# First token group of an attention-and-MLP kernel: order written out by hand, identity products ahead of it, first weights moved ahead of the last tokens

## The chip, the cores and the metric

The kernel runs on one core of one Trainium2 chip. The metric is the device time of one launch in microseconds (us). Three runs of the kernel before gave 675.87, 676.16 and 676.73 us; the median is 676.16 us. All positions below are microseconds from the start of the span of one profiled execution.

## The reference

A linear attention with decay (4 batches, 8 heads, 768 tokens, 64 columns per head) feeds a two-layer block on 3072 tokens (512 to 2048 to 512):

```python
for b in range(nb):                                   # blocks of tokens
    intra = einsum(qb, kb) * Dmask;  intra = einsum(intra, vb)
    inter = einsum(qb * lam_pow, kv_state)
    out[block] = intra + inter
    kv_state = lam_block * kv_state + einsum(kb * rev_pow, vb)
x = out as (B*S, H*D)
h = x @ w_in;  g = h - tanh(h);  result = g @ w_out
```

q, k, v are 32-bit floats. The weights arrive as 64-bit words and are turned into 32-bit floats on the chip.

## The kernel before, in words

The 768 tokens of each batch are cut into six groups of 128 (`g`); one group holds 4 batches x 128 = 512 tokens. A pair (g, b) is called a chunk here. Group 0 is done plainly; the later groups use schemes with fewer products, whose factors are built while group 0 runs. The change touches group 0 only.

**Loads (SP's queue).** `load_natural` (L123) issues q, k and v of a chunk, 256 KB each; chunk (0,3) is loaded in the order q, v, k. `load(B)` (L273) puts all four chunks of group 0 into the queue, then `load_weights(WAHEAD)` (L274) puts the first four blocks of `w_in`, 512 KB each: blocks 0 and 1 as one DMA each (L199), blocks 2 and 3 as two halves each (L202). Four buffers (`raw64`) hold raw blocks, so a later block is issued when the rounding of an earlier one has read its buffer. q has 2 buffers, k 3, v 4.

**Attention of a chunk.** `att_transpose` (L285): four TensorE transposes of q and four of k into two PSUM banks (`tp`), each copied out by ScalarE (`qt`, `kt`, L299). `att_scores` (L306): eight products into two banks (`sp`), then two VectorE multiplies by the decay mask (`ss`, L317). `att_state` (L320), for two chunks: VectorE scales k in place (L328), sixteen products (`kv`, L333), one ScalarE copy (`state`, L340). `att_out` (L342), for two chunks: sixteen products (`op`, L364) into two banks, then two ScalarE copies to `xt` (L368). `xt[0, 0]` holds chunks 0 and 1, `xt[0, 1]` chunks 2 and 3. All these use one ring of four PSUM banks (`att`).

**Rounding of a weight block.** `round_block` (L251) is two ScalarE operations, `r` (L261) and the absolute value into `w` (L263), then four VectorE operations: a maximum (L264), a shift with a mask (L266), the sign (L268), and the addition of `r` (L270). `r` has two buffers.

**The first layer.** `up_plain(u, c)` (L722), for unit u of 512 hidden columns and quarter c, sums the four input tiles i into one PSUM bank. Input tile i of unit u is weight block 4u + i. Quarters 11 and 21 read `xt[0, 0]`; 12 and 22 read `xt[0, 1]`. Sixteen quarter-steps follow, then the second layer `down_plain` (L736) with parts of group 1's attention in between.

**Order.** A scheduler sets each engine's order from the program; only operations given to `tc.keep_in_program_order` stay where they are written. In group 0 nothing is kept. Every engine works through its own queue strictly in that order. As built, TensorE's order before is:

```
tp(0,0) sp(0,0) tp(0,1) kv(0,0) sp(0,1)x2 kv(0,1) sp(0,1)x6 op(0,1)x10
tp(0,2)q x1 op x6 tp(0,2) rest, sp(0,2) tp(0,3) kv(0,2) sp(0,3)x1 kv(0,3) sp(0,3)x7
op(2,3)x10 h x1 op(2,3)x6 h ...
```

Of the kernel before, what the change touches and what calls it, by code (L numbers as in the profile page):

```python
# [23 lines left out]
def kernel(  # L24
# [90 lines left out]

    lam_blk = fwd[:, :, BLK - 1:BLK][:, None, :, :].to_broadcast([128, 2, NP, D])


    raw, late = {}, {}
    chunks = [(g, b) for g in range(NG) for b in range(B)]  # L120
    at = {"loaded": 0}

    def load_natural(g, b, names):  # L123
        for name, src, bufs in (("q", q, 2), ("v", v, 4), ("k", k, 3)) if (g, b) == (0, B - 1) else (
                ("q", q, 2), ("k", k, 3), ("v", v, 4)):
            if name in names:
                x = (qpool if name == "q" else io).tile([128, H, D], F32, name=f"{name}_nat", tag=name, bufs=bufs)
                op = nc.sync.dma_start(out=x, in_=src[b, :, ts(g, BLK), :].rearrange("h s d -> s h d"))
                if g >= GB:
                    tc.keep_in_program_order(op)  # L130
                raw[g, b][name] = x

    def load_blocks(g, b, names):
# [57 lines left out]
    ready = {"loaded": 0, "done": 0}  # L191
    wraw, pair = {}, {}

    def load_block(eng, dst, kind, n, m):

        if kind == "out":
            eng.dma_start(out=dst, in_=moe_w_out[ts(m * KH + n, 128), :].rearrange("k (a n) -> k a n", a=2))  # L197
        elif m < 2:
            eng.dma_start(out=dst, in_=w_in_u[ts(m, 128), :, ts(n, 256)])  # L199
        else:  # L200
            for j in range(2):
                eng.dma_start(out=dst[ts(1 - j, 64)], in_=w_in_u[ts(2 * m + j, 64), :, ts(n, 256)])  # L202

    def load_weights(n):

        while ready["loaded"] < min(n, len(blocks)):
            if moe_w_in.dtype != F32:
                raw64 = stage.tile([128, 2, 256], I64, name="raw64", tag="raw64", bufs=WAHEAD)
                block = blocks[ready["loaded"]]
                load_block(nc.sync if block[0] == "in" else nc.gpsimd, raw64, *block)  # L210
                wraw[ready["loaded"]] = raw64
            ready["loaded"] += 1

    def weights(n):

        while ready["done"] < min(n, len(blocks)):
            at_ = ready["done"]
            load_weights(at_ + WAHEAD)
            kind, n_, m = blocks[at_]
            if kind == "out" and m == 0:  # L220
                pair[n_] = wst.tile([128, 8, 256], F32, name="wt", tag="w")
            w = w1[n_][:, m] if kind == "in" else pair[n_][:, 2 * m:2 * m + 2]
            if at_ in wraw:
                round_block(w, wraw.pop(at_))
            else:
                load_block(nc.gpsimd, w, kind, n_, m)
            ready["done"] += 1
# [20 lines left out]
            nc.gpsimd.dma_start(out=fine[:, SUB.index(x), :, kt // 2, :].rearrange("n p c -> p n c"),  # L248
                                in_=wt[:, 3:8, ts(j, 128)])

    def round_block(w, raw64):  # L251


        word = raw64.rearrange("p a n -> p (a n)").bitcast(U32).rearrange("p (n w) -> p n w", w=2)
        wordf = raw64.rearrange("p a n -> p (a n)").bitcast(F32).rearrange("p (n w) -> p n w", w=2)
        lo, hi = word[:, :, 0], word[:, :, 1]
        w = w.rearrange("p a n -> p (a n)")
        wb, wi = w.bitcast(U32), w.bitcast(I32)

        r = stage.tile([128, 512], I32, name="r", tag="r", bufs=2)  # L260
        nc.scalar.activation(r, lo, AF.Copy, scale=2.0 ** -29)  # L261

        nc.scalar.activation(w, wordf[:, :, 1], AF.Abs)  # L263
        nc.vector.tensor_scalar(out=w, in0=w, scalar1=CLAMP, scalar2=None, op0=AL.max)  # L264

        nc.vector.tensor_scalar(out=wb, in0=wb, scalar1=3, scalar2=0x3FFFFFF8, op0=AL.logical_shift_left,  # L266
                                op1=AL.bitwise_and)
        nc.vector.scalar_tensor_tensor(out=wb, in0=hi, scalar=0xC0000000, in1=wb, op0=AL.bitwise_and,  # L268
                                       op1=AL.bitwise_or)
        nc.vector.tensor_tensor(wi, wi, r, op=AL.add)  # L270


    load(B)  # L273
    load_weights(WAHEAD)  # L274


    state = const.tile([128, B, NP, D], F32)

    def bank(name, tag, bufs):
        return psum.tile([128, 512], F32, name=name, tag=tag, bufs=bufs)  # L280


    tr, sc, kdec, xt = {}, {}, {}, {}
# [1 line left out]
    def att_transpose(g, bs):  # L285
        for b in bs:
            load(g * B + b + 1)
            t = raw[g, b]
            qt = work.tile([128, NP, BLK], F32, name="qt", tag="qt")
            kt = work.tile([128, NP, BLK], F32, name="kt", tag="kt")  # L290
            for dst, x in ((qt, "q"), (kt, "k")):
                if g >= GB:
                    tc.keep_in_program_order(nc.vector.transpose(out=dst.rearrange("d p i -> d (p i)"),
                                                                 in_=t[x + "b"].rearrange("d p r a -> d (p r a)")))
                else:
                    tp = bank("tp", "att", 4).rearrange("d (p s) -> d p s", p=NP)
                    for p in range(NP):
                        nc.tensor.transpose(out=tp[:, p, :], in_=t[x][:, 2 * p:2 * p + 2, :], identity=ident)  # L298
                    nc.scalar.activation(dst, tp, AF.Copy)  # L299
            qd = None  # L300
            if g > 0:
                qd = work.tile([128, NP, BLK], F32, name="qd", tag="qd")
                nc.vector.tensor_tensor(qd, qt, fwd, op=AL.mult)
            tr[g, b] = (qt, kt, qd)

    def att_scores(g, bs):  # L306
        for b in bs:
# [2 lines left out]
            sp = [bank("sp", "att", 4).rearrange("s (p i) -> s p i", p=NP) for _ in range(2)]  # L310
            for p in range(NP):
                for j in range(2):
                    nc.tensor.matmul(out=sp[j][:, p, :], lhsT=kt[ts(j, 64), p, :], rhs=qt[ts(j, 64), p, :],  # L313
                                     start=True, stop=True)
            ss = work.tile([128, 2, NP, BLK], F32, name="ss", tag="ss")
            for j in range(2):
                nc.vector.tensor_tensor(ss[:, j], sp[j], mask[:, j], op=AL.mult)  # L317
            sc[g, b] = ss

    def att_state(g, bs):  # L320
        if g == NG - 1:
# [2 lines left out]
        kv = bank("kv", "att", 4).rearrange("d (b p e) -> d b p e", b=2, p=NP)  # L324
        for n, b in enumerate(bs):
            kd, vn = raw[g, b]["k"], raw[g, b]["v"]
            kp = kd.rearrange("s (p j) d -> s p j d", j=2)
            kd_op = nc.vector.tensor_tensor(kp, kp, bwd, op=AL.mult)  # L328
            if g >= GB:
                tc.keep_in_program_order(kd_op)  # L330
            for p in range(NP):
                for j in range(2):
                    nc.tensor.matmul(out=kv[ts(j, 64), n, p, :], lhsT=kd[:, 2 * p + j, :], rhs=vn[:, 2 * p + j, :],  # L333
                                     start=n == 0 and p == 0, stop=True, skip_group_check=True)
        st = state[:, bs[0]:bs[0] + 2]
        if g > 0:
            nc.vector.tensor_tensor(st, st, lam_blk, op=AL.mult)
            nc.vector.tensor_tensor(st, st, kv, op=AL.add)
        else:
            nc.scalar.activation(st, kv, AF.Copy)  # L340

    def att_out(g, bs):  # L342
        half = bs[0] // 2
# [16 lines left out]
        for n, b in enumerate(bs):  # L360
            ss, vn = sc.pop((g, b)), raw[g, b]["v"]
            for p in range(NP):
                for j in range(2):
                    nc.tensor.matmul(out=dst(n, p, j), lhsT=vn[:, 2 * p + j, :], rhs=ss[:, j, p, :],  # L364
                                     start=g == 0 and n == 0 and p % 2 == 0, stop=n == 1 and p % 2 == 1,
                                     skip_group_check=True)
        for x in range(2):
            nc.scalar.activation(xt[g, half][:, 2 * x:2 * x + 2, :].rearrange("d p (b s) -> d p b s", b=2), ops[x], AF.Copy)  # L368

    def att_sums(g, bs):  # L370
        x0, x1 = xt[g, 0], xt[g, 1]
# [347 lines left out]
            nc.sync.dma_start(out=rows[:, m, c0:c1], in_=o[:, m, c0:c1])  # L719


    def up_plain(u, c):  # L722
        a, t = divmod(c - 11, 10)
        h = bank("h", ("ya", "yb", "z", "w")[2 * t + a], 1)
        hm = h.rearrange("q (m c) -> q m c", m=2)
        for m in range(2):
            for i in range(KI):
                nc.tensor.matmul(out=hm[:, m, :], lhsT=w1[u][:, i, a, ts(m, 128)], rhs=xt[0, t][:, i, :],  # L728
                                 start=m == 0 and i == 0, stop=i == KI - 1, skip_group_check=True)
        th = work.tile([128, 2, HB], F32, name="th", tag="th")  # L730
        nc.scalar.activation(th, hm, AF.Tanh)
        nc.vector.tensor_tensor(hidden(0, c)[:, u], hm, th, op=AL.subtract)

    obank = {}

# [17 lines left out]
        for fn, *args in pieces:  # L753
            fn(*args)

    for bs in ((0, 1), (2, 3)):
        for b in bs:
            att_transpose(0, (b,))
            if b == 3:
                weights(1)  # L760
            if b % 2:
                att_state(0, bs)
            att_scores(0, (b,))
        if bs[0]:
            weights(2)
        att_out(0, bs)
    weights(KI)
    for u in range(NU):
        for c in (11, 21, 12, 22):
            up_plain(u, c)  # L770
            weights(ready["done"] + 1)
        if u == 1:
            powers()
    p0, p1 = attention(1)
# [112 lines left out]
```

## Time and profile before

| what | value |
|---|---|
| median of 3 runs | 676.16 us (675.87 to 676.73) |
| time of the profiled execution | 674.97 us |
| its span, first to last instruction | 673.2 us |
| TensorE busy | 661.3 us (98% of the span) |
| VectorE, ScalarE, GpSimd busy | 481.1, 194.9, 199.9 us |
| mean granted TensorE clock | 1.000 |

Read the busy time as an average over very different stages: the first 26 us hold group 0's attention, where all engines wait for loads and for each other, and the rest is products back to back. One `nc.tensor.matmul` in 32-bit floats appears as two rows in the trace, for example 256 rows of `h` for 128 calls; a transpose appears as one row.

### The profile page before, as it was taken

The numbers are of one execution on the slowest core, as the hardware profiler recorded it, in microseconds if no ns is written. First come the engines' busy times: TensorE is split into PE (matmuls) and PEld (weight loads), VectorE is DVE, ScalarE is ACT, GpSimd is POOL, SyncE is SP. The second block draws the span as 40 slices with busy tenths as digits, with TensorE's granted clock in tenths as the row PEclk, the third lists the DMA queues.
The fourth block names the chain that finished last, engine by engine and source line by source line (L and its number), as shares of the span: only waits on it lengthen the run. The fifth ranks groups of instructions, "written<-read, shape, count | busy, mean of one in ns | idle before, by whom it ended". The sixth has DMA issues, their size and how long they took to land.

```text
span 673.2 us, 12843 instructions
## 1 busy us (share of the span) xinstructions
PE 661.3 (98%) x4808; PEld 574.9 (85%) x4808; DVE 481.1 (71%) x872; ACT 194.9 (29%) x373; POOL 199.9 (30%) x345
## 2 busy tenths in 40 slices
PE   6899999999999999999999999999999999999998
PEld 5788855558888999988999988899988899988897
DVE  3797858894887872399896378888358978347753
ACT  2764432423321111333112343112333112334110
POOL 0001414216432334144355200254300244400251
PEclk9999999999999999999999999999999999999999
DMA  9869978958855878487998741598840676610385
GB/s 187 228 210 238 288 216 256 298 145 253 264 140 125 240 200 214 115 246 214 250 281 255 198 82 44 148 284 243 250 83 5 153 244 200 231 48 0 110 302 168
DMA packets 162717, 128.80 MB, mean 191 GB/s; under 512 B 133856, under 2 KB 135008, under 8 KB 162656
## 3 DMA queue, kind: packets, MB, share of 16 engines
q0 software_dynamic: 28976, 96.49, 44.5%
q1 hardware_dynamic: 133536, 31.50, 23.5%
q8 instruction: 38, 0.62, 0.4%
q14 instruction: 23, 0.19, 0.1%
q10 hardware_dynamic: 144, 0.00, 0.0%
HBM read 103.55 MB, written 24.38 MB: 190 GB/s over the span
## 4 chain that ended last, share of the span: by engine, by line
PE 95%; DMA 2%; issue 1%; DVE 1%; ACT 0%; SPq 0%; POOL 0%; POOLq 0%; DVEq 0%
PE y L415 16%; PE y L677 11%; PE z L415 10%; PE h L728 8%; PE op L744 8%; PE zw L677 8%; PE w L624 5%; PE y L624 5%; PE y L499 4%; PE sp L313 3%; PE plain L624 3%; PE op L364 3%; PE z L499 2%; PE op L358 1%; PE kv L333 1%; PE tp L298 1%
## 5 line engine op out<-in xcount | busy, mean ns | idle before, releaser
L589 POOL DMA_DIRECT2D wb<-fine x147 | 79.2, 539 | 113.3 <-PE y L677 48.5
L423 ACT ACTIVATE th<-g 128x512 f32<-128x512 f32 x76 | 47.6, 630 | 98.7 <-DVE g L428 33.2
L592 POOL DMA_DIRECT2D wb<-factors x56 | 30.2, 541 | 153.9 <-PE y L624 97.3
L415 PE MATMUL y<-xt,w 128*128 128x256 f32 x320 | 74.0, 380 | 0.0
L415 PEld LDWEIGHTS y<-xt,w 128*128 128x128 f32 x320 | 59.9, 190 | 9.0 <-ACT g L503 0.9
L424 DVE TENSOR_TENSOR g<-g,th 128x512 f32<-128x512 f32 x76 | 51.9, 689 | 18.2 <-ACT th L423 18.1
L680 ACT ACTIVATE q<-y 128x128 f32<-128x128 f32 x84 | 23.3, 278 | 128.7 <-PE y L677 127.0
L744 PE MATMUL op<-wt,g 128*128 128x512 f32 x128 | 56.5, 595 | 0.0
L728 PE MATMUL h<-xt,w 128*128 128x256 f32 x256 | 56.1, 381 | 0.0
L728 PEld LDWEIGHTS h<-xt,w 128*128 128x128 f32 x256 | 48.3, 190 | 7.3 <-issue 0.3
L677 PE MATMUL y<-wb,g 128*128 128x128 f32 x384 | 51.1, 278 | 0.0
L744 PEld LDWEIGHTS op<-wt,g 128*128 128x128 f32 x128 | 23.8, 190 | 27.7 <-issue 26.5
L677 PEld LDWEIGHTS y<-wb,g 128*128 128x128 f32 x384 | 46.4, 192 | 1.2 <-issue 0.3
L415 PE MATMUL z<-xt,ws 128*128 128x256 f32 x160 | 38.0, 380 | 0.0
L415 PE MATMUL z<-tt,ws 128*128 128x256 f32 x160 | 38.0, 380 | 0.0
L415 PE MATMUL y<-tt,ws 128*128 128x256 f32 x160 | 37.8, 379 | 0.0
L317 DVE TENSOR_TENSOR ss<-sp,mask 128x512 f32<-128x512 f32 x48 | 31.0, 684 | 8.4 <-PE sp L313 8.4
L624 PE MATMUL y<-wb,g 128*128 128x256 f32 x160 | 35.6, 379 | 0.5 <-DVE g L434 0.5
L197 POOL DMA_DIRECT2D raw<-in_moe_w_out_dram x16 | 8.8, 553 | 91.5 <-DMA raw<-in_moe_w_in_dram 53.3
L624 PE MATMUL w<-wb,g 128*128 128x256 f32 x160 | 35.8, 382 | 0.0
L624 PEld LDWEIGHTS y<-wb,g 128*128 128x128 f32 x160 | 30.3, 190 | 5.0 <-PE y L415 0.9
L415 PEld LDWEIGHTS z<-xt,ws 128*128 128x128 f32 x160 | 30.2, 190 | 4.7 <-DVE g L446 0.4
(169 smaller groups left out, 1301.4 us busy)
## 6 DMA issues: line engine op xcount, KB each, us to landing
wb<-fine POOLq DMA_DIRECT2D x147, 256.0 KB, 3.8
wb<-factors POOLq DMA_DIRECT2D x68, 256.0 KB, 4.1
raw<-in_moe_w_out_dram POOLq DMA_DIRECT2D x16, 512.0 KB, 5.1
v_nat<-in_v_dram SPq DMA_DIRECT2D x24, 256.0 KB, 5.6
factors<-wt POOLq DMA_DIRECT2D x8, 768.0 KB, 5.5
wb<-fine_in POOLq DMA_DIRECT2D x24, 256.0 KB, 4.1
k_nat<-in_k_dram SPq DMA_DIRECT2D x20, 256.0 KB, 5.2
raw<-in_moe_w_in_dram SPq DMA_DIRECT2D x8, 512.0 KB, 5.5
```

What stands on the lines that cost most here:

```text
L317: nc.vector.tensor_tensor(ss[:, j], sp[j], mask[:, j], op=AL.mult)
L415: nc.tensor.matmul(out=t[:, m, :], lhsT=wt[:, kt, ts(m, 128)], rhs=x[:, kt, :], start=first and m == 0 and kt == 0, stop=kt == 1, skip_gro ...
L423: nc.scalar.activation(th, src, AF.Tanh)
L424: nc.vector.tensor_tensor(dst(c), src, th, op=AL.subtract)
L499: nc.tensor.matmul(out=dst[:, ts(u, 128)], lhsT=a, rhs=b, start=x in (1, 2, 5) and u == 0, stop=True, skip_group_check=True)
L589: nc.gpsimd.dma_start(out=t.rearrange("p m c -> p (m c)"), in_=fine[TWICE.index(n_), SUB.index(x_)].rearrange("p u c -> p (u c)"))
L592: nc.gpsimd.dma_start(out=t, in_=factors[XAT[FACT[n_][1]]][:, 2 * x_:2 * x_ + 2, :])
L624: nc.tensor.matmul(out=t[:, m, :], lhsT=a[:, u, kt, ts(m, 128)], rhs=wb[:, kt, :], start=first and u == 0 and m == 0 and kt == 0, stop=u = ...
L677: nc.tensor.matmul(out=dst, lhsT=a[:, u, :], rhs=wb[:, ts(u, 128)], start=x in (1, 2) and u == 0, stop=u == NU - 1, skip_group_check=True)
L680: nc.scalar.activation(keep, dst, AF.Copy)
L728: nc.tensor.matmul(out=hm[:, m, :], lhsT=w1[u][:, i, a, ts(m, 128)], rhs=xt[0, t][:, i, :], start=m == 0 and i == 0, stop=i == KI - 1, ski ...
L744: nc.tensor.matmul(out=obank[b], lhsT=g, rhs=wt[:, 2 * a:2 * a + 2, :], start=kt == 0 and a == 0, stop=kt == KH - 1 and a == 1)
```

## The change

It keeps nearly all of group 0 and of the rounding's first steps for units 0 and 1 in written order, and writes that order anew:

```diff
-        for name, src, bufs in (("q", q, 2), ("v", v, 4), ("k", k, 3)) if (g, b) == (0, B - 1) else (
-                ("q", q, 2), ("k", k, 3), ("v", v, 4)):
+        for name, src, bufs in (("q", q, 2), ("k", k, 3), ("v", v, 4)):
...
-                if g >= GB:
-                    tc.keep_in_program_order(op)
+                tc.keep_in_program_order(op)
...
+    load(B - 1)
+    load_weights(2)
     load(B)
     load_weights(WAHEAD)
+    idle = bank("idle", "w", 1)
+    for _ in range(8):
+        nc.tensor.matmul(out=idle[:, 0:128], lhsT=ident, rhs=ident, start=True, stop=True)
...
-    def up_plain(u, c):
+    def up_plain(u, cs):
...
+        for i in range(KI):
+            for c in cs:
+                a, t = divmod(c - 11, 10)
+                for m in range(2):
+                    tied(u == 0, nc.tensor.matmul(
+                        out=hm[c][:, m, :], lhsT=w1[u][:, i, a, ts(m, 128)], rhs=xt[0, t][:, i, :],
+                        start=m == 0 and i == 0, stop=i == KI - 1, skip_group_check=True))
+            if i + 1 < KI:
+                yield
...
+    for b in (0, 1):
+        att_transpose(0, (b,))
+        att_decay(0, b)
+        att_scores(0, (b,))
+    att_state(0, (0, 1))
+    att_transpose(0, (2,))
+    att_decay(0, 2)
+    weights(1)
+    att_out(0, (0, 1))
+    att_scores(0, (2,))
+    half = up_plain(0, (11, 21))
+    next(half)
+    weights(2)
+    att_transpose(0, (3,))
+    att_decay(0, 3)
+    att_scores(0, (3,))
+    next(half)
+    weights(KI)
+    att_state(0, (2, 3))
+    att_out(0, (2, 3))
+    next(half)
+    weights(KI + 2)
+    every(half)
+    weights(2 * KI)
+    every(up_plain(0, (12, 22)))
+    for u in range(1, NU):
         for c in (11, 21, 12, 22):
-            up_plain(u, c)
+            every(up_plain(u, (c,)))
             weights(ready["done"] + 1)
+        if u == 2:
+            load(2 * B)
```

`tied(yes, op)` is `tc.keep_in_program_order(op)` where `yes` holds. `att_decay` is the scaling of k, taken out of `att_state`.

As built, the queues of the first stage then read as follows (raw*n* is weight block n, round*n* its four VectorE operations, h*i* the four products of input tile i for quarters 11 and 21, u1b*n* block n of unit 1):

```
SP   q,k,v of (0,0) (0,1) (0,2), raw0, raw1, q,k,v of (0,3), raw2, raw3, unit 1's blocks ...
PE   8 identity products, tp0 sp0 tp1 sp1 kv(0,1) tp2 op(0,1) sp2 h0 tp3 sp3 h1 kv(2,3) op(2,3)
     h2 h3, then 16 products of quarters 12 and 22, then unit 1
DVE  mask x8, decay0 ss0 decay1 ss1 decay2 round0 ss2 round1 decay3 ss3 round2 round3,
     u1b0 (4), u1b1 max, g11, u1b1 shift, g21, u1b1 sign, u1b2 max, u1b1 add, u1b2 shift, sign, add,
     u1b3 max, u2b0 max, u1b3 shift, u2b0 shift, u1b3 sign, g12, u1b3 add ...
ACT  qt0 kt0 qt1 kt1 state(0,1) qt2 kt2 r0 w0 xt0 x2 r1 w1 qt3 kt3 r2 w2 r3 w3 state(2,3) xt1 x2
     r,w of u1b0 and u1b1, tanh of 11 and 21, r,w of u1b2 and u1b3, w of u2b0 ...
```

In SP's queue, the group 1 loads still follow all of `w_in`; those of chunks (1,2) and (1,3) now stand as q, k, v each, where before k and v of (1,2) and v of (1,3) came ahead of their q. GpSimd issues one more raw block of `w_out` before the first store of factors. From the second layer on, TensorE's order is as before.

More of the change, by code (lines that the diff above doesn't have):

```diff
@@ L116, with tied @@
     lam_blk = fwd[:, :, BLK - 1:BLK][:, None, :, :].to_broadcast([128, 2, NP, D])
+    def tied(yes, op):
+        return tc.keep_in_program_order(op) if yes else op
     raw, late = {}, {}
@@ L192, with load_block @@
     wraw, pair = {}, {}
-    def load_block(eng, dst, kind, n, m):
+    def load_block(eng, dst, kind, n, m, first=False):
         if kind == "out":
@@ L198, in load_block @@
         elif m < 2:
-            eng.dma_start(out=dst, in_=w_in_u[ts(m, 128), :, ts(n, 256)])
+            tied(first, eng.dma_start(out=dst, in_=w_in_u[ts(m, 128), :, ts(n, 256)]))
         else:
             for j in range(2):
-                eng.dma_start(out=dst[ts(1 - j, 64)], in_=w_in_u[ts(2 * m + j, 64), :, ts(n, 256)])
+                tied(first, eng.dma_start(out=dst[ts(1 - j, 64)], in_=w_in_u[ts(2 * m + j, 64), :, ts(n, 256)]))
     def load_weights(n):
@@ L209, in load_weights @@
                 block = blocks[ready["loaded"]]
-                load_block(nc.sync if block[0] == "in" else nc.gpsimd, raw64, *block)
+                load_block(nc.sync if block[0] == "in" else nc.gpsimd, raw64, *block, block[0] == "in")
                 wraw[ready["loaded"]] = raw64
@@ L223, in weights @@
             if at_ in wraw:
-                round_block(w, wraw.pop(at_))
+                round_block(w, wraw.pop(at_), at_ < 2 * KI)
             else:
@@ L249, in sums_out, with round_block @@
                                 in_=wt[:, 3:8, ts(j, 128)])
-    def round_block(w, raw64):
+    def round_block(w, raw64, first):
         word = raw64.rearrange("p a n -> p (a n)").bitcast(U32).rearrange("p (n w) -> p n w", w=2)
@@ L260, in round_block @@
         r = stage.tile([128, 512], I32, name="r", tag="r", bufs=2)
-        nc.scalar.activation(r, lo, AF.Copy, scale=2.0 ** -29)
-        nc.scalar.activation(w, wordf[:, :, 1], AF.Abs)
-        nc.vector.tensor_scalar(out=w, in0=w, scalar1=CLAMP, scalar2=None, op0=AL.max)
+        tied(first, nc.scalar.activation(r, lo, AF.Copy, scale=2.0 ** -29))
+        tied(first, nc.scalar.activation(w, wordf[:, :, 1], AF.Abs))
+        tied(first, nc.vector.tensor_scalar(out=w, in0=w, scalar1=CLAMP, scalar2=None, op0=AL.max))
         nc.vector.tensor_scalar(out=wb, in0=wb, scalar1=3, scalar2=0x3FFFFFF8, op0=AL.logical_shift_left,
@@ L270, in round_block, with bank @@
         nc.vector.tensor_tensor(wi, wi, r, op=AL.add)
+    def bank(name, tag, bufs):
+        return psum.tile([128, 512], F32, name=name, tag=tag, bufs=bufs)
+    load(B - 1)
+    load_weights(2)
     load(B)
     load_weights(WAHEAD)
+    idle = bank("idle", "w", 1)
+    for _ in range(8):
+        nc.tensor.matmul(out=idle[:, 0:128], lhsT=ident, rhs=ident, start=True, stop=True)
     state = const.tile([128, B, NP, D], F32)
-    def bank(name, tag, bufs):
-        return psum.tile([128, 512], F32, name=name, tag=tag, bufs=bufs)
     tr, sc, kdec, xt = {}, {}, {}, {}
@@ L297, in att_transpose @@
                     for p in range(NP):
-                        nc.tensor.transpose(out=tp[:, p, :], in_=t[x][:, 2 * p:2 * p + 2, :], identity=ident)
-                    nc.scalar.activation(dst, tp, AF.Copy)
+                        tied(g == 0 or p == 0, nc.tensor.transpose(out=tp[:, p, :], in_=t[x][:, 2 * p:2 * p + 2, :],
+                                                                   identity=ident))
+                    tied(g == 0, nc.scalar.activation(dst, tp, AF.Copy))
             qd = None
@@ L312, in att_scores, with att_decay @@
                 for j in range(2):
-                    nc.tensor.matmul(out=sp[j][:, p, :], lhsT=kt[ts(j, 64), p, :], rhs=qt[ts(j, 64), p, :],
-                                     start=True, stop=True)
+                    tied(g == 0, nc.tensor.matmul(out=sp[j][:, p, :], lhsT=kt[ts(j, 64), p, :],
+                                                  rhs=qt[ts(j, 64), p, :], start=True, stop=True))
             ss = work.tile([128, 2, NP, BLK], F32, name="ss", tag="ss")
             for j in range(2):
-                nc.vector.tensor_tensor(ss[:, j], sp[j], mask[:, j], op=AL.mult)
+                tied(g == 0, nc.vector.tensor_tensor(ss[:, j], sp[j], mask[:, j], op=AL.mult))
             sc[g, b] = ss
+    def att_decay(g, b):
+        kp = raw[g, b]["k"].rearrange("s (p j) d -> s p j d", j=2)
+        tied(g != 1, nc.vector.tensor_tensor(kp, kp, bwd, op=AL.mult))
     def att_state(g, bs):
@@ L326, in att_state @@
             kd, vn = raw[g, b]["k"], raw[g, b]["v"]
[L327 to L330, printed above, removed]
+            if g > 0:
+                att_decay(g, b)
             for p in range(NP):
                 for j in range(2):
-                    nc.tensor.matmul(out=kv[ts(j, 64), n, p, :], lhsT=kd[:, 2 * p + j, :], rhs=vn[:, 2 * p + j, :],
-                                     start=n == 0 and p == 0, stop=True, skip_group_check=True)
+                    tied(g == 0, nc.tensor.matmul(out=kv[ts(j, 64), n, p, :], lhsT=kd[:, 2 * p + j, :],
+                                                  rhs=vn[:, 2 * p + j, :], start=n == 0 and p == 0, stop=True,
+                                                  skip_group_check=True))
         st = state[:, bs[0]:bs[0] + 2]
@@ L339, in att_state @@
         else:
-            nc.scalar.activation(st, kv, AF.Copy)
+            tied(True, nc.scalar.activation(st, kv, AF.Copy))
     def att_out(g, bs):
@@ L363, in att_out @@
                 for j in range(2):
-                    nc.tensor.matmul(out=dst(n, p, j), lhsT=vn[:, 2 * p + j, :], rhs=ss[:, j, p, :],
-                                     start=g == 0 and n == 0 and p % 2 == 0, stop=n == 1 and p % 2 == 1,
-                                     skip_group_check=True)
+                    tied(g == 0, nc.tensor.matmul(out=dst(n, p, j), lhsT=vn[:, 2 * p + j, :], rhs=ss[:, j, p, :],
+                                                  start=g == 0 and n == 0 and p % 2 == 0,
+                                                  stop=n == 1 and p % 2 == 1, skip_group_check=True))
         for x in range(2):
-            nc.scalar.activation(xt[g, half][:, 2 * x:2 * x + 2, :].rearrange("d p (b s) -> d p b s", b=2), ops[x], AF.Copy)
+            tied(g == 0, nc.scalar.activation(
+                xt[g, half][:, 2 * x:2 * x + 2, :].rearrange("d p (b s) -> d p b s", b=2), ops[x], AF.Copy))
     def att_sums(g, bs):
@@ L719, in down_end @@
             nc.sync.dma_start(out=rows[:, m, c0:c1], in_=o[:, m, c0:c1])
-    def up_plain(u, c):
[L723 to L732, printed above, removed]
+    def up_plain(u, cs):
+        hm = {}
+        for c in cs:
+            a, t = divmod(c - 11, 10)
+            hm[c] = bank("h", ("ya", "yb", "z", "w")[2 * t + a], 1).rearrange("q (m c) -> q m c", m=2)
+        for i in range(KI):
+            for c in cs:
+                a, t = divmod(c - 11, 10)
+                for m in range(2):
[4 more added lines that the diff above has]
+                yield
+        for c in cs:
+            th = work.tile([128, 2, HB], F32, name="th", tag="th")
+            nc.scalar.activation(th, hm[c], AF.Tanh)
+            nc.vector.tensor_tensor(hidden(0, c)[:, u], hm[c], th, op=AL.subtract)
+        yield
     obank = {}
@@ L754, in run @@
             fn(*args)
[L756 to L766, printed above, removed]
-    weights(KI)
-    for u in range(NU):
+    for b in (0, 1):
[15 more added lines that the diff above has]
+    next(half)
+    weights(KI)
+    att_state(0, (2, 3))
[6 more added lines that the diff above has]
+    for u in range(1, NU):
         for c in (11, 21, 12, 22):
-            up_plain(u, c)
+            every(up_plain(u, (c,)))
             weights(ready["done"] + 1)
+        if u == 2:
+            load(2 * B)
         if u == 1:
```

## The prediction

> **What bounds the kernel now.** I read the page first, then busy time by stage, then the chain of waits, then the timeline of the first 45 us.
>
> ```profile
> span 673.2 us, 12843 instructions
> PE 661.3 (98%) x4808; PEld 574.9 (85%) x4808; DVE 481.1 (71%) x872; ACT 194.9 (29%) x373; POOL 199.9 (30%) x345
> ```
>
> TensorE is busy nearly always, so a gain must come from fewer products or from the few microseconds in which it waits. The same by stage (after the stretch and its length: PE, PEld, DVE, ACT and POOL busy with their rows, clock, DMA share, GB/s):
>
> ```profile
> 5.00:26.00 21.00, 18.21 (x208) 14.83 (x208) 11.41 (x23) 9.87 (x18) 0.00 (x0) 1.00 1.15 236
> 26.00:41.30 15.30, 15.23 (x80) 12.80 (x81) 14.72 (x30) 10.46 (x18) 0.00 (x0) 1.00 0.69 210
> 41.30:83.20 41.90, 41.90 (x195) 36.65 (x194) 35.70 (x79) 21.43 (x36) 8.87 (x14) 1.00 0.89 248
> ```
>
> From 26 us on there is no hole to speak of. The chance lies before: 5 us in which nothing has landed, then 21 us with 18.2 us of rows, many of them slow. VectorE is full from 26 to 41 us (14.72 of 15.30); keep that in mind. The chain shows what released TensorE at the end of the stage:
>
> ```profile
> 14.27 1.16 SPq L199
> ...
> 15.48 7.26 DMA raw<-in_moe_w_in_dram
> ...
> 22.76 0.69 ACT r L261
> 23.45 0.58 ACT w L263
> ...
> 25.41 0.61 DVE ss L317
> ...
> 26.07 0.44 PE op L364 x4
> 26.51 0.63 PE h L728 x2
> 27.14 0.81 PE op L364 x12
> 27.94 55.30 PE h L728 x254
> ```
>
> A weight block issued behind all tokens lands at 22.7 us; its rounding stands among chunk 3's mask multiplies; only then do `op(2,3)` and the products run. The last row is one unbroken stretch to 83.24 us. From there on the kernel is a rigid train: when the train starts decides the end.
>
> The timeline gives clock and latencies:
>
> ```profile
> 5.07 1.09 PE L298 MATMUL tp<-ident,q_nat 128*128 128x128 f32 x4 [5.07 <-DMA q_nat<-in_q_dram]
> ...
> 11.88 0.96 PE L333 MATMUL kv<-v_nat,k_nat 128*64 128x64 f32 x16
> ...
> 13.19 0.69 PE L333 MATMUL kv<-v_nat,k_nat 128*64 128x64 f32 x16
> ...
> 20.18 0.69 ACT L261 ACTIVATE r<-raw 128x512 int32<-128x512 uint32 x1 [1.25 <-DMA raw<-in_moe_w_in_dram]
> ...
> 42.83 2.24 PEld L728 LDWEIGHTS h<-xt,w 128*128 128x128 f32 x11 [0.31 <-DVE w L270]
> ```
>
> The same products take 0.96 us at 11.9 and 0.69 us at 13.2: TensorE ran at half rate until some 12.2 us (transposes every 0.22 us early, every 0.11 us late), although the page's clock row says full speed throughout. Block 0 landed at 20.1 us. The last row says that even before, unit 1's block 3 was ready only as the products reached it.
>
> **The change part by part.** *Nothing leaves the train.* A unit has 64 rows of 0.2177 us (55.7 us for 256), 13.93 us; units 1 to 3 take 41.8 us, so unit 0 ends now at 83.24 - 41.8 = 41.45 us. I look for that point after.
>
> *Loads.* Nine token DMAs keep their places; SP issues them every 1.1 us and is done with the ninth at 10.5 us. Then block 0 goes out, at 14.27 us before. It then took 5.9 us to land, with some 566 KB unmoved ahead of it; at 10.5 us some 596 KB are unmoved (2359 KB issued, 1763 moved), so I take 16.2 us. Block 1 took 7.3 us; issued at 11.7, it lands by 19. q, k, v of chunk 3 fall behind two blocks: k needs k(0,0)'s buffer, free after `kv(0,1)`'s first half at about 13 us, before SP gets there. With 1.05 MB more ahead (3 us at the 330 GB/s of 18 to 20 us) they land at about 19, 20 and 21 us. Blocks 2 and 3 end the same 5.24 MB as now: about 23.3 and 25.
>
> *Identity products.* Eight calls, sixteen rows, start when the identity is made (1.31 us) and take 16 x 0.22 = 3.5 us at half rate (128x128 products come every 0.111 us at full rate: `zw`, eight rows in 0.89): 1.4 to 4.9 us, in time in which TensorE has nothing. If they lasted to 5.2 they would delay only q's transposes, and k lands at 6.17. Their worth is the clock. *The trace:* full speed came 7.1 us after the first transpose. Counted from the first product that is 8.5 us. *The rule:* the Trainium skill (TensorE: Matmul & The Clock Gate, "Part 1: The HAM clock gate") wants one whole window of about 3.4 us of sustained work, and the window runs freely; "Part 4: PE-mode transpose" adds that transposes don't count as busy in the same way. 3.5 us fill one window only if the phase fits, so by the rule the products may buy nothing and full speed comes at about 12 as now. Price: at half rate until 12.2 my walk below ends at 40.05, else at 39.5. Anything up to 8.7 gives the same 39.5, since k1's landing (4.66 + 5.4, about 10.1 us) holds the transposes. Gain and nothing bound it, 0.55 and 0; I take the gain, by the trace.
>
> *The walk (full speed from 8.7 us at the latest).* kt0 is out at 7.9 at the latest, sp0 ends by 9.5; tp1 ends at 10.6; kt1 11.35. sp1 (1.16 us as at 18.98) 11.4 to 12.55. kv(0,1) 0.95: 13.5. tp2 0.9: 14.4. op(0,1) 1.9 us: 16.3, its mask multiplies done at 13.9. sp2: 17.5. TensorE now waits for round0: block 0 at 16.2, ScalarE r and w 0.59 + 0.67, VectorE 0.45 + 0.45 + 0.73 + 0.69 (starts and end of one serial block from 28.07 to 29.94): 19.75. xt0 has gone out between, by 18.4. h0 1.74: 21.5. tp3 0.9; its copy (0.6, behind the transposes) lets sp3 start at 23.3: 24.45. h1 (round1: `ss2` until 20.84, then 2.3, 23.16, early enough): 26.2. kv(2,3), op(2,3): 29.05. h2, h3: 32.5. Quarters 12 and 22, 6.97: 39.5. In all 25.0 us of work from 11.4 and two waits, 2.25 and 0.9.
>
> *Added waits.* h0 stands ahead of tp3 in TensorE's queue, so a late round0 delays everything behind it, 1 for 1. On ScalarE r0 and w0 stand ahead of xt0, r1 and w1 ahead of qt3; xt0 is needed with round0 anyway, and qt3 not before 22. On VectorE each round is one serial block, 2.24 us apart against 1.9 us where two are interleaved, and round0 stands ahead of ss2 (needed late). VectorE's line: round0 19.7, ss2 20.9, round1 23.1, decay3 23.8, ss3 24.5 to 25.8, round2 28.0, round3 30.26; h3 wants round3 at 30.85. Slack 0.6.
>
> *Unit 1.* Its first product comes at 39.5, so block 3 is wanted at 39.5 + 6 x 0.435 = 42.1 us. VectorE goes on from round3 without a pause: u1b0 to 33.5, then in its order u1b1, u1b2, two tanh subtractions (0.6 each), and u1b3 with two steps of unit 2's block 0 and one more subtraction ahead of its end: about 42.2. The unit 2 step wants its raw block: buffer free at 32.8, landing 5.7 later, 38.5, ScalarE 0.7, 39.2, against 39.0 wanted. So a stall of 0 to 0.5, 0.25 taken. After it, units 2 and 3 have some 2 us of slack (unit 3's last round ended at 67.2; it will be wanted at 70.2).
>
> *The rest.* Input tiles as the outer loop: the same rows, no cost; it moves unit 1's want of block 3 from 1.3 to 2.6 us after its start. A delayed k, v of chunks (1,2), (1,3): SP reaches them at 90.6 when q's buffer is free; their transposes are at 118 us, cover of 25 us. On GpSimd one `w_out` block goes ahead of the first two stores of factors (70 and 76 us now); factors are first read at 158 us: nothing. Both cost nothing unless the transfers queue for over 20 us.
>
> **Sum.** 41.45 - 39.5 - 0.25 = 1.7 us. Profiled execution: 674.97 = 673.2 + 1.77 around the span; after 671.5 + 1.77 = 673.3. The median stands 1.19 above the profiled one; with that kept, 674.5 us. About 0.2%, 1.35 us, can be told from no change.
>
> **The rivals.**
> *A, as above:* 1.4 to 2.2 us gained. Chance 0.42.
> *B, the blocks land sooner.* If a landing follows its last byte by the 1.25 us of the tokens instead of 1.45 to 2.5, block 0 is there at 15.4, round0 at 18.9, and TensorE waits 0.8 less: 2.5 us gained, 673.6. For: the chain to TensorE had slack in nothing but the blocks. Against: 5.9 and 7.3 us measured. 0.15.
> *C, the wait only changes its name.* The clock stays low till 12, or block 0 lands at 17, or VectorE is the bound and unit 1 stalls for a microsecond: each takes 0.5 to 1; gain 0.3 to 1.3, about 675.4. For: VectorE was already full from 26 to 41 us, and serial rounds make it slower. 0.33.
> *D, slower: the products of block 0 hold up the tokens.* h0 stands ahead of tp3, with round0 behind a landing. Before, no transpose stood behind a weight. Each microsecond after 16.2 delays all; at 17.9 the gain is gone, at 19.3 the kernel is slower by 1.4 (677.6). Against: that is 8.8 us from issue, more than any here (7.3). A share for what the walk leaves out lies here too. 0.10.
> That the change doesn't do what it says: the built order has it, so no.
>
> **How the numbers follow.** Faster by over 0.2%: most of A (0.38), B (0.15), a part of C (0.07): 0.60. Slower: D, 0.10. The same: 0.30. Likeliest 674.5; its own range 674.0 to 674.8. For 8 in 10: down to 672.9, past B, with the run-to-run spread of 0.9; up to 676.5, C and the beginning of D.
>
> **What would show it.** Right: rows of `idle` from 1.4 to 4.9, `kv` at 0.69 us per sixteen rows before 13 us; first r at 16.2, first `h` row at 19.8 with VectorE's addition (L271) as releaser; the stretch of `h` ending at 81.3 to 81.7 instead of 83.24; the rest shifted whole. Wrong: `h` waiting past 21 us, transposes of chunk 3 waiting for a token DMA, a wait of over 1 us in unit 1, or a new hole after 83 us.

## The result, and the profile after

Ten runs of the kernel after gave a median of 674.35 us (673.36 to 676.17), ten of the kernel before on the same chip 676.09 us (674.97 to 677.19). The ratio is 0.9977, with a 95% interval of 0.9966 to 0.9988: faster by 0.23%, 1.74 us. The profiled execution took 673.91 us; its span is 672.1 us, against 673.2 before.

The page's head, then busy time by stage (each line has the stretch, its length, busy time and rows of PE, PEld, DVE, ACT and POOL, then clock, DMA share and GB/s):

```profile
span 672.1 us, 12866 instructions
...
PE 660.7 (98%) x4824; PEld 575.6 (86%) x4824; DVE 480.8 (72%) x872; ACT 194.3 (29%) x373; POOL 199.9 (30%) x345
```

```profile
5.00:26.00 21.00, 15.37 (x176) 12.85 (x176) 13.60 (x25) 9.04 (x16) 0.00 (x0) 1.00 1.14 236
26.00:41.30 15.30, 15.20 (x121) 12.97 (x120) 13.99 (x28) 10.96 (x20) 0.00 (x0) 1.00 0.69 210
41.30:83.20 41.90, 41.90 (x192) 36.15 (x191) 34.99 (x78) 21.76 (x37) 8.81 (x14) 1.00 0.83 229
```

TensorE is as full as before from 26 us on. In the first stage it is busy 15.37 us instead of 18.21, and does more in that time: the rows are fewer (176 against 208), but 16 of them are the large rows of `h`, and all are at full rate. Most of the waiting is gathered in one place. The chain of waits shows what set the start of the long stretch of products:

```profile
13.85 3.37 SPq L130
...
17.27 2.22 SPq L203
...
19.53 5.74 DMA raw<-in_moe_w_in_dram
...
25.43 0.67 ACT r L262
26.11 0.57 ACT w L264
...
28.35 0.69 DVE w L271
...
30.60 0.70 DVE w L271
...
31.34 50.34 PE h L745 x232
```

The releaser of the last unbroken stretch of `h` is now VectorE's addition of block 3 (30.60), behind the rounding of block 2, which landed at 25.27 us. Ahead of block 2, SP's queue stood on one 256 KB load, v of chunk (0,3), which took 3.37 us to issue. The stretch ends at 31.34 + 50.34 = 81.68 us, against 83.24 before: 1.56 us of gain. I call this point the end of the head, and all behind it the tail.

TensorE's timeline of the head (start, duration, line, rows, and in brackets the idle time ahead and what ended it):

```profile
1.36 3.69 PE L285 MATMUL idle<-ident 128*128 128x128 f32 x16 [1.36 <-POOL ident masks.py:199]
4.96 0.66 PE L306 MATMUL tp<-ident,q_nat 128*128 128x128 f32 x4
...
7.52 1.16 PE L322 MATMUL sp<-qt,kt 64*128 64x128 f32 x16 [0.69 <-ACT kt L308]
...
12.26 1.15 PE L344 MATMUL kv<-v_nat,k_nat 128*64 128x64 f32 x32
...
19.76 1.97 PE L745 MATMUL h<-xt,w 128*128 128x256 f32 x8 [2.34 <-DVE w L271]
21.57 0.60 PE L306 MATMUL tp<-ident,q_nat 128*128 128x128 f32 x4
...
23.40 1.16 PE L322 MATMUL sp<-qt,kt 64*128 64x128 f32 x16 [0.80 <-ACT kt L308]
24.49 1.99 PE L745 MATMUL h<-xt,w 128*128 128x256 f32 x8
...
29.25 4.09 PE L745 MATMUL h<-xt,w 128*128 128x256 f32 x16
```

The transposes run at full speed from 5 us on, and `sp` takes 1.16 us instead of 2.08. The one large wait is the 2.34 us ahead of `h` of block 0. The span gained only 1.1 us of the 1.56, since the two tails differ: before lost some 0.5 us at 442 us to a transfer of factors, after lost some 0.9 us to another at 643 us (a wait of 0.6 us and slower rows behind it) and 0.25 us later.

### The profile page after: what moved, and what is told of

It reads as the page before. It is cut to its first block, busy times and chain, and to the rows that moved or that the text cites. A ratio compares the mean times of both kernels' runs of the same rounds, so it can differ in the third digit from the quotient of the medians.

```text
span 672.1 us, 12866 instructions
## 1 busy us (share of the span) xinstructions
PE 660.7 (98%) x4824; PEld 575.6 (86%) x4824; DVE 480.8 (72%) x872; ACT 194.3 (29%) x373; POOL 199.9 (30%) x345
## 4 chain that ended last, share of the span: by engine, by line
PE 87%; issue 7%; DMA 2%; SPq 1%; POOL 1%; DVE 1%; ACT 0%; POOLq 0%; ACTq 0%
PE y L428 14%; PE y L690 11%; PE op L766 8%; PE z L428 8%; PE zw L690 8%; PE h L745 7%; PE w L637 4%; PE y L637 4%; PE y L512 4%; PE plain L637 3%; PE sp L322 3%; PE op L376 3%; PE z L512 2%; PE op L370 2%; PE kv L344 1%
## 5 line engine op out<-in xcount | busy, mean ns | idle before, releaser
L693 ACT ACTIVATE q<-y 128x128 f32<-128x128 f32 x84 | 23.3, 278 | 129.8 <-PE y L690 127.8
```

Of the source, the lines that this page charges most:

```text
L693: nc.scalar.activation(keep, dst, AF.Copy)
```

## The experiments

Three measurements had four kernels each, on three chips; the kernel before ran with each (medians 676.57 us in 20 runs beside e1 to e4, 677.4 in 59 beside e5 to e8, 676.95 in 28 beside e9 to e12). The changed kernel itself did not run beside e5 to e8. Positions are of the one profiled execution of each kernel; the tail is its span less the end of the head. The time is the median of the runs.

| kernel | first `h` | end of head | tail | time, us | ratio to before |
|---|---|---|---|---|---|
| before | 26.44 | 83.24 | 590.0 | (above) | 1 |
| after, as first measured | 19.76 | 81.68 | 590.4 | 674.35 | 0.9977 [0.9966, 0.9988] |
| e1_same | 19.97 | 83.13 | 589.9 | 673.99 | 0.9963 [0.9949, 0.9976] |
| e2_no_products | 22.20 | 83.75 | 590.7 | 675.52 | 0.9981 [0.9971, 0.9992] |
| e3_tokens_first | 23.80 | 86.81 | 590.1 | 680.58 | 1.0061 [1.0045, 1.0078] |
| e4_v_last | 18.91 | 80.77 | 590.2 | 672.71 | 0.9944 [0.9933, 0.9956] |
| e5_filled | 20.03 | 83.14 | 593.8 | 676.34 | 0.9983 [0.9971, 0.9995] |
| e6_loads_only | 22.54 (2 rows) | 82.99 | 593.9 | 676.53 | 0.9979 [0.9966, 0.9993] |
| e7_no_split | 28.22 | 83.74 | 591.3 | 675.98 | 0.9982 [0.9972, 0.9993] |
| e8_untied | 25.02 | 86.17 | 597.0 | 687.16 | 1.0161 [1.012, 1.0203] |
| e9_same | 19.99 | 81.55 | 590.3 | 675.11 | 0.997 [0.9957, 0.9982] |
| e10_loads_only | 22.85 (2 rows) | 83.31 | 590.2 | 675.07 | 0.997 [0.9952, 0.9988] |
| e11_v_last | 18.96 | 81.00 | 590.2 | 673.78 | 0.9946 [0.9925, 0.9967] |
| e12_abs_first | 18.37 | 80.64 | 591.1 | 673.94 | 0.9949 [0.9931, 0.9968] |

**The changed kernel again (e1_same, e9_same).** No edit.

> The changed kernel itself, for comparison on the same chip. All theories: 674.0 to 674.8 us, 1.2 to 2.2 us under the kernel before; the unbroken stretch of products of the first layer ends at 81.5 to 82.0 us (81.68 in its first profile, 83.24 before).

> The changed kernel once more, as the mark for the three beside it. If the spread between its runs comes from the wait ahead of the first products of block 0 (2.34 us), some runs again show a granted clock of 0.997 and are about 1 to 1.5 us longer than those at 1.0. Expected: 0.9963 to 0.9980 of the kernel before.

Both ratios agree with the first. The head of e1 does not: it ends at 83.13 us, not at 81.5 to 82.0. Its timeline of TensorE, and its first stage:

```profile
16.46 1.16 PE L322 MATMUL sp<-qt,kt 64*128 64x128 f32 x16
19.97 3.58 PE L745 MATMUL h<-xt,w 128*128 128x256 f32 x8 [2.34 <-DVE w L271]
```

```profile
5.00:26.00 21.00, 15.74 (x167) 12.81 (x168) 12.71 (x24) 9.30 (x17) 0.00 (x0) 0.92 1.12 233
```

After the same 2.34 us of waiting the eight rows of `h` took 3.58 us instead of 1.97, and the granted clock of the stage is 0.92. With the head's end at 83.13, all of the gain in the head is gone. Clocks of single runs tell how often: 0.997 in 25 of the 37 runs of this kernel (6 of 10, 3 of 7, 16 of 20), 0.999 or 1.0 in the others. The kernel before showed 0.997 or less in 8 of its 107 runs in the experiments. In e9's runs the 16 at 0.997 have a median of 675.44 us and the other four 673.57; in e1's, three have 674.79 and four 673.15. So the runs with a drop are 1.6 to 1.9 us longer there (0.6 in the first measurement: 674.62 against 674.02). That e1's profile shows the drop in this wait doesn't show it for every such run.

**Without the identity products (e2_no_products).**

```diff
-    idle = bank("idle", "w", 1)
-    for _ in range(8):
-        nc.tensor.matmul(out=idle[:, 0:128], lhsT=ident, rhs=ident, start=True, stop=True)
```

> The changed kernel without the eight identity products. Theory (the blocks of weights set the start of the stretch, the clock matters little): the transposes of chunk 0 come every 0.22 us again, full speed from some 12 us; the first product of the first layer at 20.3 us (19.76 with them), block 2's landing near 25.3 still sets the end, so the stretch ends at 81.9 to 82.2: 0.2 to 0.5 us lost, about 674.8. Rival (the clock is the gain): the whole 1.6 us goes, the stretch ends at 83 or later, 675.9 or more.

The head ends 2.07 us later than after's, as the rival said. The time, 1.53 us above e1's, lies nearer to the rival's than to the theory's. The products are worth more than the prediction's 0 to 0.55. TensorE's timeline says why:

```profile
7.95 2.08 PE L319 MATMUL sp<-qt,kt 64*128 64x128 f32 x16 [0.69 <-ACT kt L305]
9.96 1.12 PE L303 MATMUL tp<-ident,q_nat 128*128 128x128 f32 x4
10.87 1.06 PE L303 MATMUL tp<-ident,k_nat 128*128 128x128 f32 x4
12.62 2.08 PE L319 MATMUL sp<-qt,kt 64*128 64x128 f32 x16 [0.69 <-ACT kt L305]
14.63 1.97 PE L341 MATMUL kv<-v_nat,k_nat 128*64 128x64 f32 x32
16.53 0.81 PE L303 MATMUL tp<-ident,q_nat 128*128 128x128 f32 x4
```

Full speed comes at some 16.8 us, not at some 12.5 as in the kernel before. There the work from 7.98 us went on unbroken, because scheduled `kv` products filled the time in which `kt` was copied; in the tied order it breaks off at 11.9 for 0.69 us, and full speed came 4.2 us after it began again at 12.62. The moment is not fixed, though. The first sixteen rows of `kv` in the old order (0.69 us at full speed), in e6's and in e10's profile, where the work began at 7.98 and 7.95 us as well:

```profile
11.83 0.69 PE L333 MATMUL kv<-v_nat,k_nat 128*64 128x64 f32 x16
```

```profile
11.86 1.12 PE L333 MATMUL kv<-v_nat,k_nat 128*64 128x64 f32 x16
```

With before's 0.96 us between them, full speed came 4.0, 4.5 and 6.0 us after the start of one and the same order (from the distances between rows). So the 2.07 us of head are those of one execution; in others e2 may lose less or more. In all ten profiles of kernels with the products `sp` of chunk 0 takes 1.16 us.

**All tokens ahead of the weights (e3_tokens_first).**

```diff
-    load(B - 1)
-    load_weights(2)
     load(B)
     load_weights(WAHEAD)
```

> The changed kernel with all tokens of group 0 loaded ahead of the first weight block, as before. Theory (the hand-written order stands or falls with block 0's landing, which the products of tile 0 await ahead of chunk 3's transposes): block 0 lands at 20.1 instead of 16.0, the first product comes at 23.8, chunk 3 follows behind it, the stretch ends at 84.5 to 85.5: 1.3 to 2.3 us slower than before, 677.4 to 678.4. Rival (the order alone is the gain, the loads are hidden anyway): within 0.5 us of the changed kernel, 674.9 or less.

Slower than before by 4.0 us: this is the prediction's rival D. ScalarE, then TensorE:

```profile
20.07 0.66 ACT L262 ACTIVATE r<-raw 128x512 int32<-128x512 uint32 x1 [4.91 <-DMA raw<-in_moe_w_in_dram]
```

```profile
23.80 3.43 PE L743 MATMUL h<-xt,w 128*128 128x256 f32 x8 [6.40 <-DVE w L271]
27.06 0.60 PE L304 MATMUL tp<-ident,q_nat 128*128 128x128 f32 x4
```

Block 0 is there at 20.07 us, `h` waits 6.40 us, and chunk 3's transposes, whose tokens have long landed, wait behind it until 27.06. The half rate after the wait adds 1.5 us, which was not in the expectation; the head ends at 86.81, later than expected. The clock was 0.992 to 0.995 in all six runs.

**v of chunks 2 and 3 last (e4_v_last, e11_v_last).** v is needed only by `kv` and `op`, late in each pair of chunks; it goes behind the first four weight blocks.

```diff
-    load(B - 1)
+    for b in range(B - 1):
+        raw[0, b] = {}
+        load_natural(0, b, "qkv" if b < 2 else "qk")
     load_weights(2)
-    load(B)
+    raw[0, 3] = {}
+    load_natural(0, 3, "qk")
     load_weights(WAHEAD)
+    load_natural(0, 2, "v")
+    load_natural(0, 3, "v")
+    at["loaded"] = B
```

> The changed kernel with v of chunks 2 and 3, which nothing reads before 26 us, loaded behind all four weight blocks. Theory (after the change the landings of blocks 0 and 2 are what TensorE waits for): block 0 lands at about 15, the first product of the first layer comes at 18.8 instead of 19.76, block 2 before 23 instead of 25.3, and the stretch ends at 80.4 to 81.0: 0.7 to 1.3 us faster than the changed kernel, about 673.4. Rival (VectorE's serial rounds and unit 1's rounding bound it already): the first products come earlier, but a wait in unit 1 takes it back, stretch ends within 0.3 us of 81.68.

> The changed kernel with v of chunks 2 and 3 behind the first four weight blocks, once more, beside the changed kernel itself. Theory: block 0 lands 0.9 us earlier, the wait ahead of its products is 1.6 us instead of 2.3 and the clock stays at 1.0 in every run: 1.0 to 1.5 us under the changed kernel's median, stretch of h ending at 80.8. Rival: the difference of the first call was the spread from run to run: within 0.5 us of the changed kernel.

```profile
15.14 0.69 ACT L262 ACTIVATE r<-raw 128x512 int32<-128x512 uint32 x1
```

```profile
18.91 1.97 PE L751 MATMUL h<-xt,w 128*128 128x256 f32 x8 [1.57 <-DVE w L271]
...
25.56 1.47 PE L350 MATMUL kv<-v_nat,k_nat 128*64 128x64 f32 x32
...
28.70 4.58 PE L751 MATMUL h<-xt,w 128*128 128x256 f32 x20
```

Block 0's rounding starts 0.87 us earlier, the wait ahead of `h` is 1.57 us (1.62 in e11), and no run of the ten had a clock below 1.0. The heads end at 80.77 and 81.00; the medians are 1.28 and 1.33 us under those of the changed kernel beside them. This version beats both kernels. Most of the 1.3 us goes with the clock: against those runs of the changed kernel that kept theirs (medians 673.15 of four and 673.57 of four) it is 0.4 us faster in e4 and 0.2 us slower in e11, with few runs in each.

**The wait filled with products (e5_filled).** Ten identity products stand ahead of `h` of block 0.

```diff
     att_scores(0, (2,))
+    for _ in range(10):
+        tied(True, nc.tensor.matmul(out=idle[:, 0:128], lhsT=ident, rhs=ident, start=True, stop=True))
     half = up_plain(0, (11, 21))
```

> The changed kernel with ten more identity products in TensorE's queue between the scores of chunk 2 and the first product of the first layer, in the wait of 2.3 us for block 0's rounding. Theory (in some runs this wait lets TensorE's clock fall to half for the 8 rows behind it, 3.58 instead of 1.97 us, which is the mean granted clock of 0.997): no run below 0.999, the first 8 rows take 1.97 us, stretch ends at 81.5 to 82.0, median 673.2 to 673.8 and less spread. Rival (the lower clock comes from elsewhere, or costs nothing): clocks of 0.997 in about half of the runs as before, and the same time as the changed kernel or some 0.2 us more.

The wait fell to 0.24 us, and only 3 of 22 runs had a clock of 0.997. The time did not follow: its ratio is that of its neighbours, and not better than those of the changed kernel elsewhere (0.9963 to 0.9977), so the expected gain is a miss. Its profile is of an execution 2.4 us above its median, and can't speak for the others: it lost 1.3 us to another wait in the head (`h` of unit 3 on a subtraction of VectorE, L753, at 75.97 us), and its tail is 3.5 us longer than e4's. The run supports the link of wait and clock, and does not show what that is worth.

**The order of the loads alone (e6_loads_only, e10_loads_only).** The kernel before, with after's `load` calls, SP order and place of `load(2 * B)`; no product or rounding is moved by hand.

```diff
+    load(B - 1)
+    load_weights(2)
     load(B)
     load_weights(WAHEAD)
...
+        if u == 2:
+            load(2 * B)
```

> The kernel before with the change's order of loads alone (SP's queue exactly as in the changed kernel, nothing else kept in order). Theory (loads and written order only work together): blocks 2 and 3 land as late as in the changed kernel (25.3, 27), tiles are needed all four at once, chunk 3's tokens land later, and the stretch ends at 83.0 to 84.5: no gain, 675.9 to 677.4. Rival (moving two blocks forward is the gain): the stretch ends by 82, 675 or less.

> The kernel before with the new order of the loads alone, once more. Theory: its products are in the old order, so the earlier blocks are worth only what its profile showed, 0.25 us (stretch of h ending at 83.0): 0.999 to 1.0 of the kernel before. Rival: its time on the other chip (ratio 0.998) is real, then 0.9985 or below here too, and something outside group 0 gains, which the chain after 83 us must show.

A miss for my theory, twice. The heads end as it said, at 82.99 and 83.31: block 0, whose rounding starts at 16.04 and 16.05 instead of 20.18, buys at most 0.25 us there, since the scheduler moves only two rows of `h` forward (to 22.54 and 22.85) and leaves the others behind the attention. Yet the times are 0.87 and 1.88 us under before. On the last chip that is as fast as the changed kernel beside it (675.07 and 675.11 us). The gain is real and not in the head. What can differ behind it shows in these two profiles of one and the same kernel. TensorE's waits after 84 us (in total, times, longest), first e6, then e10:

```profile
PE y L624 <- DVE g L434: 1.8, 1, 1.8
PE zw L677 <- DMA wb<-fine: 1.2, 2, 0.7
PE y L624 <- DMA wb<-factors: 0.9, 1, 0.9
```

```profile
PE y L624 <- PE y L415: 0.5, 1, 0.5
PE y L677 <- DMA wb<-fine: 0.5, 1, 0.5
```

3.9 us against 1.0, for tails of 593.9 and 590.2; of the 3.9, 2.1 are waits for factors (`wb`) that come back through DRAM. e6's profile is of an execution 2.2 us above its median, e10's of one at its median. The kernel before was profiled once, in the fastest of its ten runs, with the short tail. Which of its waits the new loads shorten can't be read from that, and no run here tells it.

**h of block 0 behind all attention (e7_no_split).**

```diff
-    half = up_plain(0, (11, 21))
-    next(half)
     weights(2)
...
     att_scores(0, (3,))
-    next(half)
     weights(KI)
     att_state(0, (2, 3))
     att_out(0, (2, 3))
-    next(half)
+    half = up_plain(0, (11, 21))
```

> The changed kernel with all products of quarters 11 and 21 of unit 0 behind the attention of chunks 2 and 3, instead of one input tile at a time between its parts. Theory: the 7 us of unit 0's products no longer fill waits; chunk 3's mask multiplies still follow two roundings, op(2,3) ends at about 27.6, and the stretch ends at 83.0 to 83.6: about 1.5 us lost, 675.5 to 676. Rival (the waits that the tiles fill are not on the path): within 0.4 us of the changed kernel.

```profile
16.20 1.16 PE L322 MATMUL sp<-qt,kt 64*128 64x128 f32 x16
20.13 1.09 PE L306 MATMUL tp<-ident,q_nat 128*128 128x128 f32 x4 [2.77 <-DMA q_nat<-in_q_dram]
...
22.82 2.08 PE L322 MATMUL sp<-qt,kt 64*128 64x128 f32 x16 [0.75 <-ACT kt L308]
...
28.22 5.02 PE L745 MATMUL h<-xt,w 128*128 128x256 f32 x22
```

The wait only changes its name: 2.77 us for q of chunk 3. Transposes, `sp` and most of `kv` then run at half rate in the profile (granted clock 0.50 from 20 to 26 us), and all 22 runs had a clock of 0.997 or less. The head ends at 83.74. Putting `h` of block 0 into the gap is worth 0.6 to 2.1 us of head, by whether after's own clock drops. What it is worth in time isn't shown, as the changed kernel did not run beside it; its 675.98 us are the lowest of the four.

**No operation tied (e8_untied).** `tied` returns its operation without keeping it in order. This frees the weight loads as well.

```diff
-        return tc.keep_in_program_order(op) if yes else op
+        return op
```

> The changed program with the scheduler free again: only the token loads are kept in order. It puts blocks 0 and 1 ahead of chunk 2 and their rounding ahead of chunk 0's mask multiplies in VectorE's and ScalarE's queues. Theory (each engine's queue is strict, so this order waits for a weight at 13 us before any attention): first mask multiply not before 14 instead of 8.7, the stretch ends at 84.5 to 86.5, 677.4 to 679.5. Rival (written order differs little from what the scheduler finds): within 0.7 us of the changed kernel.

```profile
12.77 0.66 ACT L262 ACTIVATE r<-raw 128x512 int32<-128x512 uint32 x1 [5.34 <-DMA raw<-in_moe_w_in_dram]
...
15.86 0.59 ACT L308 ACTIVATE kt<-tp 128x512 f32<-128x512 f32 x1
```

```profile
16.50 2.08 PE L322 MATMUL sp<-qt,kt 64*128 64x128 f32 x16 [6.11 <-ACT kt L308]
```

The scheduler puts block 0's `r` ahead of chunk 1's `kt` on ScalarE. `r` waits 5.34 us for its block, `kt` waits behind it, `sp` of chunk 1 comes at 16.50 instead of 11.17, and at half rate. The first mask multiply waits behind block 0's rounding in VectorE's queue, as expected, until 14.82 us (8.72 in after). The loss in time is larger than expected, since the tail loses too (4.4 us in one wait on `g`). So the written order is needed with this order of work.

**The absolute value ahead of r, with v last (e12_abs_first).**

```diff
-        tied(first, nc.scalar.activation(r, lo, AF.Copy, scale=2.0 ** -29))
         tied(first, nc.scalar.activation(w, wordf[:, :, 1], AF.Abs))
+        tied(first, nc.scalar.activation(r, lo, AF.Copy, scale=2.0 ** -29))
```

> As the one before, and in the rounding ScalarE makes the absolute value w ahead of r, so that VectorE's maximum, shift and sign need not wait for r. Theory: the wait ahead of the first products of block 0 shrinks by r's 0.57 us to about 1.0 us, first h at 18.3, stretch of h ending at about 80.2: 0.4 to 0.6 us under the kernel with v last alone. Rival: the last rounds or VectorE (full until 41 us) set the start of the later input tiles, not round 0: within 0.2 us of it, and a wait of h on the addition of block 2 or 3 shows up in place of the one that shrank.

```profile
18.37 1.97 PE L750 MATMUL h<-xt,w 128*128 128x256 f32 x8 [0.95 <-DVE w L270]
...
25.40 1.50 PE L349 MATMUL kv<-v_nat,k_nat 128*64 128x64 f32 x32 [0.30 <-DMA v_nat<-in_v_dram]
```

The first `h` comes at 18.37 and waits 0.95 us, as worked out. Of the 0.59 us gained on e11 there, 0.36 is left at the end of the head; `kv(2,3)` waits 0.30 us for v, 0.22 in e11. The wait on a later addition that the rival named is not there. In time it is the same as v last alone (673.94 and 673.78 us), so the expected gain did not come. Two of its six runs had a clock of 0.997 although its wait is the shorter one, so the length of that wait alone does not decide the clock.

## Why the prediction was right, and where it was not

The time (674.5 against 674.35) and the likeliest case, A, came out. That they agree within 0.15 us is partly luck: the profiled execution was put at 673.3 us and the median 1.19 us above it; they are 673.91, and 0.44 above it, and the two errors cancel. By the steps:

- *Block 0 at 16.2, first `h` at 19.75, `sp` of chunk 3 at 23.3, h1 from 24.45:* 16.01, 19.76, 23.40 and 24.49. The releaser is the addition of L271, as named. `kv(0,1)`'s rows before 13 us were at full rate.
- *Rounds 2 and 3 at 28.0 and 30.26:* 29.04 and 31.30. The term that was mis-sized is the landing of blocks 2 and 3, put at 23.3 and 25 us "as now"; they landed at 25.27 and 27.52. Most of the error is in the "now": in before's own trace they landed at 24.66 and 26.51. The further 0.6 and 1.0 us come behind the 3.37 us in which v of chunk (0,3) was issued and the 2.22 us for block 2's first half, and the DMA share fell to 0.58 from 20 to 21 us. Whether the slow issue or the order of the transfers makes them wasn't tested: in e4, with v moved away, block 2's first half itself took 3.00 us to issue, and block 2 landed at 22.00, with 512 KB of v no longer ahead of it. Block 2 was rounded from 25.43, the slack of 0.6 us that I gave VectorE was used up, and PEld waited at 31.3.
- *Unit 0's end at 39.5, a stall of 0.25 in unit 1:* 81.68 - 41.8 = 39.88 and no stall. Block 3 of unit 1 was ready at 42.19 (42.2 predicted), and with the later start it was wanted only at 39.88 + 2.61 = 42.49. The two errors nearly cancel: 1.56 us gained in the head against 1.7.
- *Identity products, 0 to 0.55 us:* wrong in size. I took from before's trace that full speed would come by 12.2 us in any case. e2 shows 16.8, and 2.07 us of head, in its one profile. The Trainium skill (TensorE: Matmul & The Clock Gate, "Part 1: The HAM clock gate") asks for a whole window of about 3.4 us of sustained work, and says that the window runs freely. The traces agree as far as they go: with the products full speed came by 5 us (after) to 8 us (e5), without them 4.0 to 6.0 us into the old order's unbroken work, and not in e2's first stretch, which was 4.0 us long. That rule, followed through the new order with its gap at 11.9 us, would have shown that more than 0.55 us was at stake. "Part 4: PE-mode transpose", which I set against the trace, mattered less: the old order reached full speed in e6 after 4.0 us of work, some 1.8 us of it transposes.
- *What I left out: the clock can be lost again.* I priced the wait ahead of `h` at its 2.25 us. In e1's execution the rows behind it also ran at half rate, 1.6 us more, and runs with such a clock are 25 of 37.
- *Loads of group 1 and of `w_out`, costed at nothing:* the loads as a whole bring 0.87 and 1.88 us that the head doesn't show (e6, e10). Where this arises stays open; the group 0 blocks and the group 1 order were not taken apart.

So the 1.74 us are not simply the 1.7 us of the sum. In a run at full clock, if its head is as in after's profile, the head gives 1.56 us and the rest comes from elsewhere: before's median less the median of such runs is 2.1 us in the first measurement (676.09 - 674.02) and 3.4 us in e1's and e9's. In a run whose clock dropped as in e1's profile the head gives 0.1 us, and the time is still 1.5 to 1.8 us under before's median, about what the loads alone give (0.87 and 1.88). The median is a mixture of the two. The size was right; the sum had one gain too few and one loss too few, and that these were of like size is luck as well.

Of the rivals, B's earlier landing did not come (16.01 us, not 15.4). C's three causes did not come in after's profile: clock and landing of block 0 were as in A, and the later rounds took 0.4 us. A clock that falls again is a cost of C's kind, though, which I had not listed. D's mechanism is real (e3), with its place and sign as described; it was not reached because block 0 landed at 16.01, and 17.9 was the point of no gain. The train after 83 us shifted whole until 421 us (by 1.56 to 1.67 us), as predicted.

## What to carry to other kernels

Ahead of a long unbroken run of products, order the loads by when each is first read: v behind the weights brought 1.3 us that the change had left, most of it in runs of the change whose clock dropped. When products are put into a gap, price the gap twice, by its length and by the clock that TensorE may lose in it, and look at the granted clock of many runs, since one profile shows one of the two cases. Ask also for a kernel that does only the cheap part of a change; here the loads alone ran as fast as the whole on the same chip.

## What the runs showed of the hardware

- A wait of TensorE of 2.3 us was followed by half rate in one profile (3.58 instead of 1.97 us for eight rows), and waits of 2.34 and 2.66 us were not in two others of the same kernel. By kernel, the longest wait of TensorE in group 0's attention once it ran at full speed, in the profile, and the runs with a clock of 0.997 or less: 0.80 us (e5, with 0.24 ahead of `h`), 3 of 22; 0.95, 2 of 6; 1.43 (e2), 0 of 14; 1.57 to 1.62, 0 of 10; 2.34 to 2.66, 25 of 37; 2.77, 22 of 22; 6.11 (e8), 6 of 6; 6.40, 6 of 6. It rises with the wait, but not strictly, and the kernels ran on different chips.
- The granted clock of the profile shows such a drop, and not the slow start: e2 ran at half rate until 16.8 us, and its stage up to 16.5 us has a clock of 1.00.
- Whether the clock had dropped could not be told from the first profile: its stage clock was 1.00, while six of the ten runs had 0.997.
- A DMA's issue can hold up SP's queue for 3.37 us (v of chunk (0,3), 13.85 us) where the same load takes 1.1 us earlier. The load itself is not the reason: in e4, with v moved away, block 2's first half takes 3.00 us at 13.32 us.
